# Output products of six batches in seven block products instead of eight, and one order table for the whole program

## The chip, the cores and the metric

One core of a Trainium2 chip runs the kernel. The metric is the device time of one execution in microseconds. Before the change it is 711.71 us, the median of three runs (711.54 to 712.73). All data is float32.

## What is computed

Attention through a few packed tokens (32 per head and batch), and behind it a feed-forward layer of two matrix products with a SiLU between them:

```python
# q, k, v: (8, 8, 576, 64); p: (8, 8, 32, 64): batch, head, token, head dim
def sm_attn(qq, kk, vv):
    s = scale * np.matmul(qq, kk.transpose(0, 1, 3, 2))
    s = s - np.max(s, axis=-1, keepdims=True)
    a = np.exp(s)
    a = a / (np.sum(a, axis=-1, keepdims=True) + 1e-09)
    return np.matmul(a, vv)
p_packed = sm_attn(p, k, v)
x = sm_attn(q, p_packed, p_packed)      # then as (8 * 576, 512)
h = x @ w_in                            # w_in: (512, 2048)
return (h / (1 + np.exp(-h))) @ w_out   # w_out: (2048, 512)
```

## The kernel before, in words

The second attention and the first product are never formed apart: `Packs` multiplies the 32 packed tokens of each head with `w_in` (`pw`, per batch and quarter of the 2048 hidden features), and the shares of the second softmax (`a2`, lines 437 to 447) times `pw` are then the hidden values. `h_products` (L502) does this for one **unit**, a batch and 128 hidden features, over the 576 tokens, in two matmuls of 288 columns (a half batch each) times six.

Six, because every factor is split in two parts, `hi` (rounded to the TensorE's float32r) and `lo` (what is left), and a product is made of three terms, hi·hi, lo·hi and hi·lo. The splitting is work of ScalarE (`hi`) and VectorE (`lo`).

`h_values` (L520 to L522) applies SiLU from PSUM: L520 writes `g`, L521 the same rounded as `g_hi`, L522 the last 32 tokens of each half (the **rest**, `REST`) to the tile `rest`. `h_lower` (L527) makes `g_lo`. `out_products` (L529 to L559) multiplies a unit's 512 main tokens, as four stationary blocks of 128 tokens, with the unit's 128 rows of `w_out`: 4 blocks x 3 terms = 12 matmuls of 512 columns, L534. The sums over a batch's 16 units stand in PSUM (`ps_acc`, two tiles of two banks, one tile for each half batch); `out_rows` copies them out (L580) and stores them. The 64 rest tokens of a batch wait until two batches give 128; four rest units of their own then take 48 matmuls of 512 columns.

The weights arrive as int64 words and are turned into float32 in the first part of the program (`Weights`, L190 to L215, on ScalarE, VectorE and GpSimd).

What sets the order: every engine runs its own list. Up to batch 1 (**the early part**, 32 units) the list is the table `ORDER`; from batch 2 on (**the main loop**, line 690) it is code: `hidden_up_to(u + 2)` makes the hidden values two units ahead of the output products, and `STEPS_AT` puts the steps of the next batch's attention between them. Loads and stores are all issued in order by the queue of SP.

Of the kernel before, what the change touches and what calls it, by code (L numbers as in the profile page):

```python
# [19 lines left out]
P = 128  # L20
# [8 lines left out]
NJ = 4  # L29
JW = DFF // NJ  # L30
# [15 lines left out]
CHUNKS += [(j * FJ + f, 2, inner) for j in range(1, NJ) for inner in (True, False) for f in (0, 2)]  # L46
PLACES = ["new", "last", "new", "last", 8, 10, 12, 14]
# [4 lines left out]
W6 k0 as0.0 wf0 wf1 ws0 W1 as0.1 am0.0 am0.1 v0 ax0.0 ax0.1 wz0 wj0 W7 at0.0 at0.1 ws1 ay0.0 ay0.1 wz1 wj1 wf2 ar0  # L52
W5 aa0 an0 wu1 wl1 W1 ai0 aj0 q0 W1 aS0.0 ws2 pp0 wz2 wj2 wf3 aC0.0 pu0 pl0 W1 aB0.0 aM0.0 ws3 wz3 aS0.1 aC0.1 pp1
wf4 aX0.0 wf5 pu1 wj3 ws5 wf6 W4 aB0.1 aM0.1 ws4 aD0.0 W13 aU0.0 aX0.1 aD0.1 wf7 ws7 wz7 pl1 k1 aH0.0 wu3 aU0.1 ws6
aH0.1 as1.0 ac1.0 wj7 v1 aL0.0 aL0.1 as1.1 ac1.1 wl3 h0.0 wz5 wj5 h0.1 am1 g0.0 g0.1 l0.0 h1.0 h1.1 l0.1 ax1.0 ax1.1
wz4 wj4 q1 at1.0 wu5 wl5 at1.1 g1.0 g1.1 ar1 l1.0 o0.0 wz6 wf8 o0.1 wf9 wf10 pp2 pu2 pl2 ws8 l1.1 o1.0 h2.0 h2.1 wj6
wz8 g2.0 ay1 l2.0 g2.1 pp3 pu3 pl3 wj8 wu7 wl7 ws9 l2.1 o1.1 wz9 wj9 h3.0 h3.1 g3.0 g3.1 l3.0 wf11 o2.0 o2.1 ws10
aa1 wf12 wf13 pp4 pu4 wz10 wj10 l3.1 ws11 wu10 an1 o3.0 o3.1 pl4 ai1 h4 aj1 wz11 wl10 g4 l4 h5 ws12 aS1.0 aT1.0
aM1.0 g5 aX1.0 wj11 o4 l5 aS1.1 aT1.1 aD1.0 h6 g6 k2 l6 wu11 h7 o5 wl11 aH1.0 aL1.0 o6 pp5 aM1.1 g7 aX1.1 pu5 l7
# [701 lines left out]
```

## Time and profile before

| | |
|---|---|
| median of the runs | 711.71 us |
| span of the profiled execution | 713.2 us |
| early part, up to the last output product of batch 1 | some 199 us |
| main loop, batches 2 to 7 | some 510 us |
| PE busy | 98% |
| VectorE and ScalarE busy | 47% each |
| moved by DMA | 65.20 MB |

PE is TensorE's matmul row, PEld its weight load, DVE VectorE, ACT ScalarE, POOL GpSimd, SP the engine that issues the loads. A matmul's duration in the profile contains its way through the array and overlaps the next, so that the distance from one start to the next tells its cost, and a long run of equal matmuls gives that distance as its length over their number. The profiled execution's span is 1.5 us above the median of the runs.

### The profile page before, as it was taken

The numbers are of one execution on the slowest core, as the hardware profiler recorded it, in microseconds if no ns is written. First come the engines' busy times: TensorE is split into PE (matmuls) and PEld (weight loads), VectorE is DVE, ScalarE is ACT, GpSimd is POOL, SyncE is SP. The second block draws the span as 40 slices with busy tenths as digits, with TensorE's granted clock in tenths as the row PEclk, the third lists the DMA queues.
The fourth block names the chain that finished last, engine by engine and source line by source line (L and its number), as shares of the span: only waits on it lengthen the run. The fifth ranks groups of instructions, "written<-read, shape, count | busy, mean of one in ns | idle before, by whom it ended". The sixth has DMA issues, their size and how long they took to land.

```text
span 713.2 us, 12182 instructions
## 1 busy us (share of the span) xinstructions
PE 696.0 (98%) x5094; PEld 571.3 (80%) x5094; DVE 333.6 (47%) x506; ACT 331.7 (47%) x619; POOL 17.0 (2%) x16
## 2 busy tenths in 40 slices
PE   7889999999999999999999999999999999999997
PEld 5667788878868887888878888888878888888886
DVE  4889876677353336332462324523462234622112
ACT  4778776555333516352442524453253532533221
POOL 0102002020000000000000000000000000000000
PEclk9789999999999999999999999999999999999999
DMA  9666452613032130212211122031401210010002
GB/s 360 269 239 248 158 206 84 247 82 119 1 133 82 33 146 1 82 58 91 74 60 38 58 91 74 11 116 35 145 1 59 82 34 2 1 60 0 1 1 74
DMA packets 30869, 65.20 MB, mean 91 GB/s; under 512 B 19296, under 2 KB 19296, under 8 KB 26464
## 3 DMA queue, kind: packets, MB, share of 16 engines
q1 hardware_dynamic: 30720, 64.30, 24.8%
q8 instruction: 40, 0.66, 0.4%
q10 hardware_dynamic: 96, 0.13, 0.1%
q14 instruction: 13, 0.11, 0.0%
HBM read 48.76 MB, written 11.53 MB: 85 GB/s over the span
## 4 chain that ended last, share of the span: by engine, by line
PE 88%; DVE 5%; ACT 2%; DMA 2%; issue 1%; POOL 0%; SPq 0%; ACTq 0%; DVEq 0%
PE ps_acc L534 54%; PE ps_two L502 27%; PE ps_two L222 6%; DMA w_raw<-in_w_out 1%; PE ps_two L320 1%; DMA w_raw<-in_w_in 1%; DVE w_raw L196 1%; DVE w_raw L195 1%; DVE win L202 1%; ACT w_raw L191 0%; DVE win L196 0%; ACT L520 0%; DVE wo_lo L215 0%; DVE g_lo L527 0%; ACT w_raw L190 0%
## 5 line engine op out<-in xcount | busy, mean ns | idle before, releaser
L534 PE MATMUL ps_acc<-wo_hi,g_hi 128*128 128x512 f32 x576 | 229.6, 399 | 0.0
L534 PE MATMUL ps_acc<-wo_lo,g_hi 128*128 128x512 f32 x576 | 225.9, 392 | 0.9 <-DVE wo_lo L215 0.9
L534 PE MATMUL ps_acc<-wo_hi,g_lo 128*128 128x512 f32 x576 | 225.5, 392 | 0.0
L527 DVE TENSOR_TENSOR g_lo<-g,g_hi 128x512 fp32r<-128x512 f32 (+1 forms) x132 | 88.6, 672 | 263.3 <-ACT g_hi L521 263.3
L520 ACT ACTIVATE g<-ps_two 128x512 f32<-128x512 f32 (+1 forms) x132 | 77.4, 587 | 267.0 <-PE ps_two L502 243.2
L502 PE MATMUL ps_two<-a_hi,pw_hi 128*128 128x288 f32 x512 | 153.3, 299 | 0.1
L502 PE MATMUL ps_two<-a_lo,pw_hi 128*128 128x288 f32 x512 | 152.6, 298 | 0.0
L502 PE MATMUL ps_two<-a_hi,pw_lo 128*128 128x288 f32 x512 | 151.7, 296 | 0.0
L534 PEld LDWEIGHTS ps_acc<-wo_hi,g_hi 128*128 128x128 f32 x576 | 108.3, 188 | 40.7 <-issue 21.0
L534 PEld LDWEIGHTS ps_acc<-wo_hi,g_lo 128*128 128x128 f32 x576 | 108.4, 188 | 24.1 <-DVE g_lo L527 0.5
L534 PEld LDWEIGHTS ps_acc<-wo_lo,g_hi 128*128 128x128 f32 x576 | 108.4, 188 | 19.7 <-DVE wo_lo L215 1.2
L502 PEld LDWEIGHTS ps_two<-a_hi,pw_hi 128*128 128x128 f32 x512 | 97.5, 190 | 6.1 <-ACT tm L248 0.9
L502 PEld LDWEIGHTS ps_two<-a_lo,pw_hi 128*128 128x128 f32 x512 | 97.2, 190 | 3.4
L502 PEld LDWEIGHTS ps_two<-a_hi,pw_lo 128*128 128x128 f32 x512 | 97.3, 190 | 0.0
L521 ACT ACTIVATE g_hi<-ps_two 128x512 fp32r<-128x512 f32 (+1 forms) x132 | 76.6, 581 | 9.4 <-PE ps_acc L534 9.4
L474 DVE TENSOR_TENSOR pw_lo<-ps_two,pw_hi 128x1024 fp32r<-128x1024 f32 (+1 forms) x35 | 38.5, 1127 | 14.6 <-ACT pw_hi L471 14.6
L471 ACT CAST pw_hi<-ps_two 128x1024 fp32r<-128x1024 f32 (+1 forms) x35 | 31.9, 943 | 24.2 <-PE ps_two L222 24.2
L222 PE MATMUL ps_two<-win,ppT 64*32 64x512 f32 (+1 forms) x560 | 33.5, 568 | 4.2 <-ACT rest L522 2.4
L522 ACT ACTIVATE rest<-ps_two 128x64 f32<-128x64 f32 (+1 forms) x132 | 30.4, 230 | 0.0
L222 PEld LDWEIGHTS ps_two<-win,ppT 64*32 64x32 f32 x560 | 8.2, 108 | 18.4 <-issue 10.8
L520 ACT ACT_TABLE_LOAD x17 | 21.8, 1283 | 2.0 <-PE ps_two L502 1.8
L190 ACT ACTIVATE w_raw<-w_raw 128x1024 int32<-128x1024 uint32 (+1 forms) x13 | 13.3, 1022 | 8.0 <-DMA w_raw<-in_w_in 5.5
(104 smaller groups left out, 445.9 us busy)
## 6 DMA issues: line engine op xcount, KB each, us to landing
kvq_t<-in_v SPq DMA_DIRECT2D x8, 1280.0 KB, 5.9
kvq_t<-in_pkT SPq DMA_DIRECT2D x7, 1216.0 KB, 7.3
out<-o SPq DMA_DIRECT2D x16, 512.0 KB, 2.8
kvq_t<-in_qT SPq DMA_DIRECT2D x7, 1152.0 KB, 5.0
w_raw<-in_w_in SPq DMA_DIRECT2D x6, 1024.0 KB, 7.0
win<-in_w_out SPq DMA_DIRECT2D x3, 1024.0 KB, 4.6
w_raw<-in_w_out SPq DMA_DIRECT2D x3, 1024.0 KB, 7.4
tm<-tm SPq DMA_DIRECT2D x56, 40.0 KB, 1.9
```

Of the source, the lines that this page charges most:

```text
L190: nc.scalar.activation(low, low.bitcast(U32), AF.Copy, scale=2.0**-29)
L195: nc.vector.tensor_scalar(up.bitcast(F32), up.bitcast(F32), TOP, -TOP, op0=ALU.min, op1=ALU.max)
L196: nc.vector.scalar_tensor_tensor(low, up, -(2**31), low, op0=ALU.bitwise_and, op1=ALU.bitwise_or)
L222: nc.tensor.matmul(bank(par)[NP * i : NP * i + NP], lhs(r, i), rhs(r, i), start=True, stop=True)
L471: nc.scalar.copy(self.hi, self.ps[:, :, : self.nf * P])
L474: nc.vector.tensor_tensor(self.lo, self.ps[:, :, : self.nf * P], self.hi.bitcast(F32), ALU.subtract)
L502: nc.tensor.matmul(bank, p[:, par, cols], a[:, par], start=(n == 0), stop=(n == len(todo) - 1))
L520: nc.scalar.activation(g, ps[..., :MAIN], AF.Silu)
L521: nc.scalar.activation(g_hi, ps[..., :MAIN], AF.Silu)
L522: nc.scalar.activation(to, ps[..., MAIN:HS], AF.Silu)
L527: nc.vector.tensor_tensor(g_lo[:, c], g[:, c], g_hi[:, c].bitcast(F32), ALU.subtract)
L534: nc.tensor.matmul(bank, g[:, rows], w[:, f], start=(first and n == 0), stop=(last and n == 2))
```

## The change

**Seven products.** For batches 2 to 7 a unit is now a half batch (256 main tokens) and a pair of 128 features. Its output product is seen as a 2 x 2 block product: two blocks of tokens by two blocks of features, times two blocks of features by two halves of 256 output columns. `pair_products` makes it with seven block products (Strassen's scheme, in the variant with four sums on each side) where the plain form has eight: 7 x 3 = 21 matmuls of 256 columns in place of 12 of 512. What goes with it:

- On the hidden values: ScalarE writes SiLU once (`pair_values`, 512 wide, and `rest_values`), GpSimd adds four sums of blocks to it (`pair_sums`, three instructions of 128, 256 and 128 columns), and `all_upper` and `all_lower` split seven blocks, 896 columns, in place of four. L521 goes away.
- On the weights: four sums per pair of features are made once in the early part (`pair_of_w`, two VectorE adds of 512 columns; `sums_of_pair`, four GpSimd instructions of 256; `sums_upper` and `sums_lower`, 1024 wide on ScalarE and VectorE), for eight pairs, and are stored to HBM. The first of them goes in the place of a part of `w_out` (`first_in_place`); the other three are read again for every unit (`load_sums`, 786 KB, four buffers, 96 times).
- In PSUM: the seven products are summed over the pairs of a half batch in four banks, `ps_acc0` to `ps_acc3`, of which there is one set. `pair_rows` joins them to the output: one ScalarE copy of 256 columns and five VectorE adds (512, 256, 256, 256 and 512). The rest units use banks 0 and 2, and `rest_rows` joins these.
- `win`, the first weights, no longer stays in SBUF: it is stored once (`w_in32`, 4 x 1 MB), and 22 quarters of 1 MB are fetched again (`Packs.fetch`).

**One table.** `ORDER` now holds the whole program, and the loop over the units is gone. Steps are cut finer (`clip`, `shift`, `scaled2`, ...), with the same instructions. The new table differs from the old from the first steps on; its rows say little to a reader, and two of its lines stand here:

```python
O41 O42 N43 I43 F43 L43 N44 B45 N45 S45 aa3 S46 G45 B46 an3 ai3 aj3 I44 F44 O43 L44 N46 E2.0 S48 G46 I45 F45 L45 B47
O139 F140 L140 E7.1 O140 F141 L141 F142 O141 F143 L142 L143 O142 O143 Y6
```

(O output products, B hidden products, G SiLU, N SiLU of the rest, I sums, F hi, L lo, S load of the weights' sums, E and Y the joining of the banks; the number is the unit's.)

```diff
+    w_in32 = tc.dram_tile((NJ, P, FJ * DM), I32, name="w_in32")
+    sums_of_w = tc.dram_tile((NPAIR, P, 2, 3 * HALF), F32, name="sums_of_w")
+    first_sums = tc.dram_tile((NPAIR, P, 2, HALF), F32, name="first_sums")
...
+    def pair_values(u):
+        g = hidden[u] = gp_main.tile([P, 8 * P], F32, name="g")
+        nc.scalar.activation(g[:, : 4 * P].rearrange("p (e s) -> p e s", e=2), made["h", u, None][..., :MAIN], AF.Silu)
...
+    def pair_sums(u):
+        x = hidden[u].rearrange("p (n x) -> p n x", x=P)
+        one = x[:, 1:2].broadcast_to([P, 2, P])
+        nc.gpsimd.tensor_tensor(x[:, 4], x[:, 0], x[:, 2], ALU.subtract)
+        nc.gpsimd.tensor_tensor(x[:, 5:7], x[:, 0:5:4], one, ALU.subtract)
+        nc.gpsimd.tensor_tensor(x[:, 7], x[:, 3], x[:, 6], ALU.add)
...
+    def all_upper(u):
+        g = all_of(u)
+        both = [gp_main.tile([P, 7 * P], F32R, name=name)[:, : g.shape[1]] for name in ("g_hi", "g_lo")]
+        hidden[u] = g, *both
+        nc.scalar.copy(both[0], g)
+    def all_lower(u):
+        g, g_hi, g_lo = hidden[u]
+        nc.vector.tensor_tensor(g_lo, g, g_hi.bitcast(F32), ALU.subtract)
...
+    def terms(out, g_hi, g_lo, at, w_hi, w_lo, first=False, last=False):
+        rows = slice(at * P, at * P + P)
+        todo = ((g_hi, w_hi), (g_hi, w_lo), (g_lo, w_hi))
+        for n, (g, w) in enumerate(todo):
+            nc.tensor.matmul(
+                out, g[:, rows], w, start=(first and n == 0), stop=(last and n == 2), skip_group_check=True
...
+    def pair_products(u):
+        b, (hf, p) = units[u]
+        g_hi, g_lo = hidden[u][-2:]
+        last = p == NPAIR - 1
+        def term(bank, cols, at, w_hi, w_lo):
+            key = "pair", b, hf, bank
+            begun = opened.get(key)
+            opened[key] = True
+            terms(acc[bank][:, cols], g_hi, g_lo, at, w_hi, w_lo, not begun, last)
+        f1, f2 = 2 * p, 2 * p + 1
+        x = summed_tiles.pop((b, hf, p))
+        t = lambda n: (x[:, 0, n * HALF : n * HALF + HALF], x[:, 1, n * HALF : n * HALF + HALF])
+        w = lambda f, c: (wo_hi[:, f, c], wo_lo[:, f, c])
+        term(1, low, 5, *t(0))
+        term(1, high, 2, *w(f2, low))
+        term(0, low, 0, *w(f1, low))
+        term(0, high, 4, *t(2))
+        term(2, low, 6, *w(f2, high))
+        term(3, low, 1, *t(1))
+        term(3, high, 3, *w(f1, high))
...
+    def load_sums(u):
+        b, (hf, p) = units[u]
+        x = summed_tiles[b, hf, p] = tp.tile([P, 2, 3 * HALF], F32R, name="sums_of_w")
+        nc.sync.dma_start(x.bitcast(F32), sums_of_w[p])
...
+    def sums_of_pair(p):
+        b11, b21, b22, b12 = (made["r", p][:, n * HALF : n * HALF + HALF] for n in range(4))
+        nc.gpsimd.tensor_tensor(b22, b12, b22, ALU.add)
+        nc.gpsimd.tensor_tensor(b12, b12, b11, ALU.subtract)
+        nc.gpsimd.tensor_tensor(b11, b11, b22, ALU.subtract)
+        nc.gpsimd.tensor_tensor(b21, b11, b21, ALU.add)
...
+    def first_in_place(p):
+        for n, t in enumerate((wo_hi, wo_lo)):
+            nc.sync.dma_start(t[:, 2 * p, high].bitcast(F32), first_sums[p, :, n])
+        summed[p] = True
...
+    def rest_rows(b):
+        o = osb.tile([P, 2, DM], F32, name="o")
+        if opened.get(("rest", b, 0)):
+            nc.scalar.copy(o[:, 1], acc[0])
+            nc.vector.tensor_tensor(o[:, 0], acc[2], o[:, 1], ALU.add)
+            nc.vector.tensor_tensor(o[:, 0, high], o[:, 0, high], o[:, 1, low], ALU.add)
...
+    def pair_rows(b, hf):
+        o = osb.tile([P, 2, DM], F32, name="o")
+        o4 = o.rearrange("p k (c x) -> p (k c) x", x=HALF)
+        banks = [x.rearrange("p (c x) -> p c x", x=HALF) for x in acc]
+        twice = lambda n: o4[:, n : n + 1].broadcast_to([P, 2, HALF])
+        add = lambda to, ps, x: nc.vector.tensor_tensor(to, ps, x, ALU.add)
+        nc.scalar.copy(o4[:, 1], banks[0][:, 0])
+        add(o4[:, 0:3:2], banks[1], twice(1))
+        add(o4[:, 1], banks[0][:, 1], o4[:, 0])
+        add(o4[:, 3], banks[3][:, 1], o4[:, 0])
+        add(o4[:, 3], banks[2][:, 0], o4[:, 3])
+        add(o4[:, 0:2], banks[3], twice(1))
+        store(b, hf, o)
```

Three places show how it moves instructions. On PE, at the end of a unit's output products in the main loop, there stood before (a plain form: ahead of the arrow what is written, behind it first the moving and then the stationary factor; `wo` is `w_out`, `pw` the packed tokens times `w_in`):

```order
L534 MATMUL ps_acc<-wo_hi,g_hi 128x512
L534 MATMUL ps_acc<-wo_lo,g_hi 128x512
L534 MATMUL ps_acc<-wo_hi,g_lo 128x512
L502 MATMUL ps_two<-a_hi,pw_hi 128x288
L502 MATMUL ps_two<-a_lo,pw_hi 128x288
L502 MATMUL ps_two<-a_hi,pw_lo 128x288
```

and now, for one unit (`ps_acc_2184` is bank 1, `2183` bank 0, `2185` bank 2; `sums_of_w` are the loaded sums of weights):

```order
L587 MATMUL ps_two<-a_hi,pw_lo 128x288
L643 MATMUL ps_acc_2184<-sums_of_w,g_hi 128x256 x2
L643 MATMUL ps_acc_2184<-sums_of_w,g_lo 128x256
L643 MATMUL ps_acc_2184<-wo_hi,g_hi 128x256
L643 MATMUL ps_acc_2184<-wo_lo,g_hi 128x256
L643 MATMUL ps_acc_2184<-wo_hi,g_lo 128x256
L643 MATMUL ps_acc_2183<-wo_hi,g_hi 128x256
L643 MATMUL ps_acc_2183<-wo_lo,g_hi 128x256
L643 MATMUL ps_acc_2183<-wo_hi,g_lo 128x256
L643 MATMUL ps_acc_2183<-sums_of_w,g_hi 128x256 x2
L643 MATMUL ps_acc_2183<-sums_of_w,g_lo 128x256
L643 MATMUL ps_acc_2185<-wo_hi,g_hi 128x256
```

The matmuls of 512 columns became more matmuls of 256, each with its own stationary block, over four banks that all units of a half batch share.

On VectorE at the end of the program there stood before (`o` is the staged output):

```order
L527 TENSOR_TENSOR g_lo_6452<-rest_93,g_hi_6451 128x512
L580 COPY o_6470<-ps_acc_5986 128x1024
L527 TENSOR_TENSOR g_lo_6474<-rest_93,g_hi_6473 128x512
L527 TENSOR_TENSOR g_lo_6491<-rest_93,g_hi_6490 128x512
L569 COPY o_6530<-ps_acc_6477 128x256
```

and now:

```order
L637 TENSOR_TENSOR g_lo<-rest,g_hi 128x512
L785 TENSOR_TENSOR o<-ps_acc_2184,o 128x2x256
L785 TENSOR_TENSOR o<-ps_acc_2183,o 128x256
L785 TENSOR_TENSOR o<-ps_acc_2186,o 128x256
L785 TENSOR_TENSOR o<-ps_acc_2185,o 128x256
L785 TENSOR_TENSOR o<-ps_acc_2186,o 128x512
L637 TENSOR_TENSOR g_lo<-rest,g_hi 128x512 x3
L770 TENSOR_TENSOR o<-ps_acc_2185,o 128x512
L771 TENSOR_TENSOR o<-o 128x256
```

The joining of a half batch's four banks, five adds, now stands between the first and the second splitting of the last rest tokens, and the last copy of 256 columns became an add of 512 and one of 256.

On the queue of SP, in the loop over the batches, there stood before (`kvq_t` takes the inputs of the next batch's attention, `tm` the turned scores):

```order
L143 DMA kvq_t_4073<-in_pkT 128x2432
L162 DMA kvq_t_4147<-in_v 128x2560
L583 DMA out<-o_4427 128x2x512
L583 DMA out<-o_4430 128x2x512
L156 DMA kvq_t_4488<-in_qT 128x2304
L299 DMA tm_4588<-tm_4585 32x5x64 x2
L299 DMA tm_4588<-tm_4585 32x4x64 x2
```

and now:

```order
L714 DMA sums_of_w_3126<-sums_of_w_104 128x1536
L714 DMA sums_of_w_3183<-sums_of_w_104 128x1536
L714 DMA sums_of_w_3185<-sums_of_w_104 128x1536
L714 DMA sums_of_w_3263<-sums_of_w_104 128x1536
L216 DMA kvq_t_3265<-in_v 128x2560
L532 DMA w_quarter_3273<-w_in32_103 128x2048
L714 DMA sums_of_w_3280<-sums_of_w_104 128x1536
L714 DMA sums_of_w_3319<-sums_of_w_104 128x1536
L764 DMA out<-o_3343 128x2x512
L210 DMA kvq_t_3357<-in_qT 128x2304
L714 DMA sums_of_w_3372<-sums_of_w_104 128x1536
L714 DMA sums_of_w_3444<-sums_of_w_104 128x1536
```

Loads of the weights' sums and of the first weights' quarters stand between the others, so that a load or a store that waits holds up the sums behind it.

## Rows read from the trace of the kernel before

**Rows 1.** The page's first two parts: busy time and share of the span of three engines, and the granted clock of PE in 40 slices (tenths).

```profile
PE 696.0 (98%) x5094; PEld 571.3 (80%) x5094; DVE 333.6 (47%) x506; ACT 331.7 (47%) x619; POOL 17.0 (2%) x16
...
PEclk9789999999999999999999999999999999999999
```

**Rows 2.** The chain that ended last, by engine.

```profile
PE 88%; DVE 5%; ACT 2%; DMA 2%; issue 1%; POOL 0%; SPq 0%; ACTq 0%; DVEq 0%
```

**Rows 3.** Windows by stage: length, busy time of each engine (and its instructions), granted clock, DMA share, GB/s.

```profile
0.00:32.00 32.00, 25.31 (x319) 18.50 (x319) 21.93 (x44) 18.84 (x35) 3.81 (x9) 0.89 0.81 329
32.00:80.00 48.00, 45.24 (x389) 34.72 (x375) 43.23 (x72) 38.11 (x68) 5.20 (x3) 0.89 0.58 217
80.00:199.00 119.00, 117.05 (x805) 97.19 (x812) 77.69 (x101) 70.00 (x116) 7.95 (x4) 1.00 0.35 126
199.00:709.00 510.00, 508.40 (x3605) 420.89 (x3589) 190.32 (x290) 204.34 (x401) 0.00 (x0) 1.00 0.17 57
```

**Rows 4.** Who waited for whom, PE alone: us in total, times, longest; the two longest of ten rows.

```profile
PE ps_two L222 <- ACT rest L522: 3.4, 2, 2.4
PE ps_acc L392 <- DVE tm L425: 1.9, 2, 1.2
```

**Rows 5.** Pieces of the chain in order of time: start, length, what, how many.

```profile
210.63 2.73 PE ps_acc L534 x12
...
226.09 3.19 PE ps_two L502 x24
...
364.68 10.95 PE ps_acc L534 x48
...
689.89 19.09 PE ps_acc L534 x84
```

**Rows 6.** Timeline of PE at 22.6 us: start, length from the first start to the last end, 26 passes of 128 columns, each behind a weight load of its own.

```profile
22.60 3.07 PE L137 MATMUL ps_two<-ident 128*128 128x128 f32 x26
```

**Rows 7.** Windows of the first slice and of that stretch, columns as in Rows 3.

```profile
0.00:17.83 17.83, 13.19 (x199) 9.88 (x199) 8.85 (x21) 8.24 (x16) 1.74 (x7) 1.00 0.91 359
22.60:25.60 3.00, 3.00 (x28) 2.88 (x26) 2.83 (x6) 3.00 (x6) 1.04 (x1) 1.00 1.01 426
```

**Rows 8.** Groups of instructions by line and form: shapes, number, busy us, mean ns of one, idle time before.

```profile
L527 DVE TENSOR_TENSOR g_lo<-g,g_hi 128x512 fp32r<-128x512 f32 x124 | 85.4, 688 | 262.5 <-ACT g_hi L521 262.5
L520 ACT ACTIVATE g<-ps_two 128x512 f32<-128x512 f32 x124 | 74.3, 599 | 262.6 <-PE ps_two L502 241.3 <-DVE g_lo L527 21.1
...
L474 DVE TENSOR_TENSOR pw_lo<-ps_two,pw_hi 128x1024 fp32r<-128x1024 f32 x31 | 36.9, 1219 | 13.2 <-ACT pw_hi L471 13.2
...
L471 ACT CAST pw_hi<-ps_two 128x1024 fp32r<-128x1024 f32 x31 | 30.4, 1016 | 24.0 <-PE ps_two L222 24.0
L522 ACT ACTIVATE rest<-ps_two 128x64 f32<-128x64 f32 x124 | 28.7, 231 | 0.0
L520 ACT ACT_TABLE_LOAD x17 | 21.8, 1283 | 2.0 <-PE ps_two L502 1.8
...
L569 DVE COPY o<-ps_acc 128x256 f32<-128x256 f32 x4 | 1.7, 424 | 11.5 <-ACT o L568 11.5
...
L568 ACT COPY o<-ps_acc 128x256 f32<-128x256 f32 x4 | 1.5, 372 | 12.4 <-PE ps_acc L534 12.4
```

**Rows 9.** Timeline of VectorE and GpSimd in two stretches (a GpSimd add of 1024 columns alone, and one beside VectorE).

```profile
106.88 1.89 POOL L203 TENSOR_TENSOR w_raw<-w_raw 128x1024 int32<-128x1024 int32 x1 [35.54 <-DVE w_raw L202]
...
144.25 0.68 DVE L527 TENSOR_TENSOR g_lo<-g,g_hi 128x512 fp32r<-128x512 f32 x1
...
144.42 2.27 POOL L203 TENSOR_TENSOR w_raw<-w_raw 128x1024 int32<-128x1024 int32 x1 [26.50 <-DVE w_raw L202]
145.21 2.03 DVE L195 TENSOR_SCALAR w_raw<-w_raw 128x1024 f32<-128x1024 f32 x1 [0.28 <-ACT w_raw L191]
```

**Rows 10.** DMA: one queue's packets, MB and share of the 16 engines' span; then issues by line: number, KB each, median us from issue to landing.

```profile
q1 hardware_dynamic: 30720, 64.30, 24.8%
...
out<-o SPq DMA_DIRECT2D x16, 512.0 KB, 2.8
...
w_raw<-in_w_in SPq DMA_DIRECT2D x6, 1024.0 KB, 7.0
...
win<-in_w_in SPq DMA_DIRECT2D x2, 512.0 KB, 13.3
```

**Rows 11.** Timeline of the last 5 us.

```profile
708.58 0.39 PE L534 MATMUL ps_acc<-wo_hi,g_lo 128*128 128x512 f32 x1
709.05 0.37 ACT L568 COPY o<-ps_acc 128x256 f32<-128x256 f32 x1 [7.81 <-PE ps_acc L534]
709.46 0.42 DVE L569 COPY o<-ps_acc 128x256 f32<-128x256 f32 x1 [7.49 <-ACT o L568]
709.91 0.80 SPq L573 DMA_DIRECT2D out<-o  x2
```

More of the change, by code (lines that the diff above doesn't have):

```diff
@@ new lines, in pair_sums, with all_of @@
+    def pair_sums(u):
[4 more added lines that the diff above has]
+        nc.gpsimd.tensor_tensor(x[:, 7], x[:, 3], x[:, 6], ALU.add)
+    def all_of(u):
+        b, f, *more = units[u]
+        if more:
+            return rest[:, f : f + FJ].rearrange("p f e h s -> p (f e h s)")
+        return hidden[u][:, P:]
@@ L529, in products @@
     def products(bank, u, f, at, first, last):
         g_hi, g_lo = hidden[u][-2:]
-        rows = slice(at * P, at * P + P)
-        todo = ((g_hi, wo_hi), (g_hi, wo_lo), (g_lo, wo_hi))
-        for n, (g, w) in enumerate(todo):
-            nc.tensor.matmul(bank, g[:, rows], w[:, f], start=(first and n == 0), stop=(last and n == 2))
+        terms(bank, g_hi, g_lo, at, wo_hi[:, f], wo_lo[:, f], first, last)
     def is_last(u):
-        return u + 1 == len(units) or units[u + 1][0] != units[u][0] or len(units[u + 1]) > len(units[u])
+        if u >= n_early:
+            return units[u][0:1] != units[u + 1][0:1] or len(units[u]) != len(units[u + 1]) if u + 1 < len(units) else True
@@ L539, in first_of @@
+        return units[u + 1][0] != units[u][0]
     def first_of(u):
@@ new lines, in packed_attention_ffn, with rest_products @@
+    low, high = slice(0, HALF), slice(HALF, DM)
+    def rest_products(u):
+        b, f, _ = units[u]
+        first, last = f == 0, f + FJ == NF
+        for n in range(FJ):
+            bank = 0 if n % 2 == 0 and (f + n) // 2 in summed else 2
+            begun = opened.get(("rest", b, bank))
+            opened["rest", b, bank] = True
+            products(acc[bank], u, f + n, n, not begun, last and n >= FJ - 2)
+    opened = {}
+    def pair_products(u):
[18 more added lines that the diff above has]
+        term(3, high, 3, *w(f1, high))
@@ L561, in out_rows @@
     def out_rows(u, h):
         b, f, *more = units[u]
-        sums = acc[first_of(u), h]
-        if more:
-            o = osb.tile([P, 2, DM], F32, name="o")
-            half = DM // 2
-            nc.scalar.copy(o[:, 0, :half], sums[:, 0, :half])
-            nc.vector.tensor_copy(o[:, 0, half:], sums[:, 0, half:])
-            for n, (e, h) in enumerate((e, h) for e in range(2) for h in range(2)):
-                at = (b + e) * S + h * HS + MAIN
-                rows = slice((2 * e + h) * REST, (2 * e + h) * REST + REST)
-                (nc.scalar if n % 2 and b == B - 2 else nc.sync).dma_start(out[at : at + REST], o[rows, 0])
-            return
+        banks = sums[first_of(u), h]
@@ L632, in packed_attention_ffn @@
-    gp_b = ent(tc.tile_pool(name="gp_b", bufs=1))
-    done = n_early
-    def hidden_up_to(u):
-        nonlocal done
-        while done < min(u, len(units) - 1):
-            done += 1
-            if len(units[done]) == 2:
-                h_products(done)
-            h_values(done)
-            h_lower(done)
-    def packs_in(b, *quarters):
-        both = [Packs(b, FJ * j, FJ) for j in quarters]
-        for part in both:
-            part.products()
-        for part in both:
-            part.upper()
-            part.lower()
@@ L720, in _laid_out @@
+    for step in ORDER.split():
+        which = step.rstrip("0123456789.") if step[0] != "Z" else step
+        steps[which](*map(int, filter(None, step[len(which) :].split("."))))
 def _laid_out(q, k, v, p, moe_w_in, moe_w_out):
```

391 lines of the change are left out of this document (224 added, 167 removed).

## The prediction, made before the changed kernel ran

> **What bounds the kernel now.** I read the page's busy times first, then the chain, then windows by stage. PE is busy 98% of the span, VectorE and ScalarE 47% each [rows 1], and 88% of the chain that ended last is PE [rows 2]. A busy PE row proves little, since matmuls overlap; so I look at who PE waited for. Its longest wait in total is 3.4 us, and the next 1.9 us [rows 4], all in the first part of the program. From 80 us on the granted clock is 1.00, the higher of the two levels (2.4 GHz), and in the main loop (199 to 709 us) PE is busy 508.4 of 510 us while VectorE works 190.3, ScalarE 204.3 and GpSimd nothing [rows 3]. The main loop is bound by PE alone: it gets shorter only if matmuls take less time, and work on the other engines is free as long as it stays ahead of PE. The first 80 us are different: there VectorE works 43.2 of 48 us and the clock is 0.89 [rows 3].
>
> **What a matmul costs.** A long run of 512 columns takes 10.95 us for 48, one unit's output products 2.73 us for 12, so 0.228 us each; 24 matmuls of 288 columns take 3.19 us, 0.133 us each [rows 5]. The difference of 0.095 us for 224 columns is 0.00042 us a column, and 288 columns at that price leave 0.011 to 0.013 us that each matmul pays whatever its width. A matmul of 256 columns is not in the trace of before. By this line it takes 0.133 - 32 x 0.00042 = 0.1194 us. From above, it can't take longer than one of 288 columns, 0.133 us, unless width is not what counts. Between these lies the weight load: each of the 26 passes of 128 columns at 22.6 us has its own load, and they come every (3.07 - 0.3) / 25 = 0.111 us at a clock of 1.00 [rows 6, 7]. By the line, 128 columns would take only 0.066 us, so there something else sets the pace, which may be the load. If a load of 0.111 us and the fixed 0.013 us were added, a matmul of 256 columns would take 0.124 us. I take 0.1194, since two rows of the same kind of matmul lie on either side of a line that has no bend between them, and keep 0.124 and 0.133 for the range.
>
> The Trainium skill ("TensorE: Matmul & The Clock Gate", Back-to-back issue gap) gives N / 2.4 + 2.5 ns for the gap, 109 ns at 256 and 216 ns at 512 columns; by that the change would save 96 x (12 x 0.2157 - 21 x 0.1092) = 28 us. The trace's 0.228 us at 512 columns speaks against it. The same page (LDWEIGHTS) puts a load of 128 columns at 128 / 1.2 = 107 ns, which is as long as 256 columns at full clock, and so speaks against narrow matmuls here; the 0.111 us between the passes agree with it.
>
> **The change, part by part.**
>
> 1. *Output products of batches 2 to 7.* For each pair of features and half batch, 96 units: before 12 x 0.2275 = 2.73 us, now 21 x 0.1194 = 2.51 us. That is 0.223 us a unit and **-21.4 us** in all, on PE, where it counts. At 0.124 it is 96 x (2.73 - 2.604) = -12.1 us, at 0.133 it is +6 us; the break-even lies at 0.130 us. One block product in eight is saved, 12.5%, but the fixed 0.013 us now falls due 21 times instead of 12, which takes 0.12 us back. Hidden products, rest units, packs and attention keep their matmuls.
>
> 2. *The other engines in the main loop.* A unit used to need 599 + 593 (L521, like L520) + 231 ns of ScalarE and 688 ns of VectorE [rows 8]. Now ScalarE does 599 + 231 ns and a split of 896 columns, about 0.91 us from the 1016 ns for 1024; VectorE splits 896, about 1.09 us from 688 and 1219 for 512 and 1024 [rows 8]. GpSimd adds 512 columns in three steps, 1.0 us and some tenths from its 1.89 us for 1024 [rows 9], if float adds cost what those of integers do. A unit with its hidden products (12 x 0.133 = 1.6 us) lasts 4.1 us on PE. Loads of about 1.7, 1.1 and 1.2 us fit with ease; with attention the sums are some 47 us of ScalarE and 46 us of VectorE in a batch of 82 us. So nothing becomes the bound by its sum. What can bite is the order: `g_hi` and `g_lo` have two buffers, so `all_upper` of unit u + 2 can't start before the output products of u are done; then 0.91 + 1.09 us and the signals have to fit under those of u + 1 (2.51 us) and often a hidden product (1.6 us). Without the latter, 2.3 to 2.4 us stand against 2.51: just enough. An exponential with its two table loads (2 x 1.28 us [rows 8]) between two such steps is late by some tenths. Eight more table loads, 34 to 42 by the program, are 10 us of ScalarE in this shadow. I set **+3 us** (bounds 0 and 96 x 0.5 = 48).
>
> 3. *GpSimd beside VectorE.* A GpSimd add of 1024 took 1.89 us alone and 2.27 us when L527, whose two inputs both lie in SBUF, overlapped its start; L527 itself took its usual 0.68 us; L195, which came behind, took 2.03 us [rows 9]. So a GpSimd step may be longer by 0.4 us next to a split. The chain SiLU, sums, hi, lo is some 3.8 us, and two units ahead PE has 6.6 us of other work. I add nothing.
>
> The Trainium skill ("GPSIMD Engine Reference", its first table) says that GpSimd shares its SBUF interfaces with VectorE, with contention for instructions with two SBUF inputs. Here it was GpSimd that paid, not L527.
>
> 4. *The ends of the 12 half batches.* There is now one set of four banks. After the last output product of a half, a copy of 0.37 us and an add of 512 columns (0.69 us) free bank 1, which the next half writes first; the rest follows at 0.42 us a step, faster than the next products reach the banks (0.72 us each). In the table a hidden product of 1.6 us stands between for 11 of the 12, so they cost nothing. Without such a cover each costs 1.2 us. The last one has none, and the rest units begin with bank 0, which is free after 0.37 + 0.69 + 0.42 us and signals: **+1.8 us**.
>
> 5. *The end.* The last copies, 0.37 and 0.42 us [rows 11], become a copy of 512, an add of 512 and one of 256: 0.6 us (between 372 and 1016 ns for 256 and 1024) + 0.69 + 0.42 us, **+0.9 us**.
>
> 6. *Loads.* Sums of 786 KB for each of 96 units, 75.5 MB, and 22 quarters, 23 MB. In a batch 12.6 + 4.2 MB come to the 5.5 MB of inputs, scores and output: 22.3 MB in 82 us, 272 GB/s. Queue 1 moved 64.30 MB in 24.8% of the span, which makes 363 GB/s for a fully busy set of engines, and in the first 17.8 us it ran at 359 GB/s at a share of 0.91 [rows 7, 10]. So the engines are busy three quarters of the time, with four buffers, three units or 12 us ahead. A load of 512 KB took 2.8 us when the queue was short, one of 1 MB 7.0 us, and 13.3 us at the start with everything queued [rows 10]. The order of SP holds sums behind waiting stores and fetches, but mostly with spare tiles already there. I set 0, and keep the other end as a rival. What I looked for and didn't find is PE slowed by DMA: at a share of 1.01 the passes in rows 6 came at full pace [rows 7].
>
> 7. *The early part.* Eight pairs of weight sums add 8 x (2 x 0.69 + 1.22) = 20.8 us of VectorE, 8 us of ScalarE, 16 us of GpSimd. From 80 to 199 us VectorE has 119 - 77.7 = 41 us free [rows 3], so this fits, closer than before. The other order may win or lose in the first 80 us: PE stood idle 2.8 of the 48 us after 32 us, and 11% of clock is missing there [rows 3], 8 us in all. The first attention has the same VectorE steps ahead of it. I set **+2 us** (bounds -8 and +20.8).
>
> Sum against the profiled execution: 713.2 - 21.4 + 3 + 1.8 + 0.9 + 2 = 699.5 us of span. The median of the runs lies 1.5 us under that execution's span, so **698.0 us**.
>
> **Rivals.**
>
> *The weight load sets the pace* (0.124 us a matmul). For it speaks the 0.111 us in rows 6; against it that the two widths in rows 5 share one line. Item 1 becomes -12.1 us: 713.2 - 12.1 + 7.7 - 1.5 = 707 us. The LDWEIGHTS section of the Trainium skill's page named above stands for this rival.
>
> *The chain behind each unit eats the gain.* If the splits come 0.23 us late on average, item 1 is gone. For it speaks the 2.4 against 2.51 us of item 2; against it the many hidden products in between. 712 to 722 us, in the middle 717.
>
> *The sums come late, and the kernel is slower.* If sums and fetches don't get 272 GB/s, DMA sets the pace from batch 2 on. For it speaks that landings took up to 13.3 us when much was queued [rows 10]; against it that 217 GB/s needed only a share of 0.58 [rows 3], 374 at a full one. At 250 GB/s a batch takes 89 us in place of 82, six times, some 42 us: 740 us. It decides from a landing of 12 us, three units.
>
> *The table also repairs the early part.* If the 8 us of item 7 come back and the splits are never late: about 688 us.
>
> *The change does not do what it says* can be left aside: the program has 2016 matmuls of 256 columns in place of 1152 of 512.
>
> **How the numbers follow.** The forecast has a chance of 0.62 (692 to 703 us, other terms of item 2 and 7); the weight load 0.12 (703 to 709); the late splits 0.10; late sums 0.06; the repaired early part 0.10 (686 to 692). The range of 690 to 712 us leaves out late sums, half of the late splits and a part of the last. A measurement of this kernel can tell 0.2%, 1.4 us, from no change. Slower than 713.1 us: late sums and 0.06 of the late splits, 0.12. Within: the other 0.04 of these. Faster than 710.3: 0.84.
>
> **What would show it.** The starts of matmuls of 256 columns 0.119 us apart show item 1 right, 0.124 or more the weight load. A main loop with PE waiting for `g_hi` or `g_lo` at L643 in total over 5 us shows item 2 wrong; waits for `sums_of_w`, item 6. One wait of near 2 us for bank 0 before the last rest units, and 5.2 us from the last matmul to the end, are items 4 and 5. The early part should still end at about 200 us. I am wrong if the narrow matmuls don't follow the line, or if PE waits often and shortly, which no sum of busy times shows.

## The result and the profile after

The changed kernel takes 695.88 us, the median of four runs (694.97 to 696.58), beside 712.21 us for the kernel before on the same chip (711.54 to 712.73): a ratio of 0.977, with a 95% interval of 0.9756 to 0.9784. The prediction was 698.0 us, in a range of 690 to 712.

The page's busy times, its main DMA queue and the chain by engine, which answer to [rows 1, 2, 10], then the groups of GpSimd's sums (number, busy us, mean ns, idle before) and the loads of the weights' sums (number, KB each, median us to landing):

```profile
PE 674.6 (97%) x5958; PEld 593.1 (85%) x5958; DVE 425.9 (61%) x588; ACT 386.5 (56%) x641; POOL 232.4 (33%) x336
...
q1 hardware_dynamic: 54944, 177.56, 69.0%
...
PE 77%; DVE 10%; ACT 4%; DMA 4%; SPq 2%; issue 2%; POOL 1%; ACTq 0%; DVEq 0%
...
L619 POOL TENSOR_TENSOR g<-g 128x128 f32<-128x128 f32 x96 | 56.4, 587 | 290.7 <-ACT g L609 290.6
...
L620 POOL TENSOR_TENSOR g<-g 128x256 f32<-128x256 f32 x96 | 75.0, 783 | 6.6
...
L621 POOL TENSOR_TENSOR g<-g 128x128 f32<-128x128 f32 x96 | 52.3, 546 | 6.6
...
sums_of_w<-sums_of_w SPq DMA_DIRECT2D x96, 768.0 KB, 6.3
```

PE is still the bound, but its share of the chain fell from 88 to 77%, although its busy share hardly changed. VectorE, ScalarE and DMA now stand in the chain in many pieces, most of them short: PE has no long wait, but much has to come just in time.

Windows by stage (length, busy time of each engine and its instructions, granted clock, DMA share, GB/s), beside [rows 3]:

```profile
32.00:80.00 48.00, 46.59 (x408) 36.24 (x408) 43.86 (x73) 38.41 (x70) 5.21 (x3) 0.98 0.63 222
80.00:200.00 120.00, 117.77 (x804) 95.04 (x810) 98.83 (x118) 72.77 (x118) 40.95 (x36) 1.00 0.67 241
200.00:690.00 490.00, 487.05 (x4469) 446.09 (x4453) 259.35 (x351) 254.74 (x419) 182.02 (x288) 1.00 0.70 260
```

The early part ends where it did, now with VectorE busy 98.83 of 120 us. The main loop is some 20 us shorter with PE still full. DMA moves 260 GB/s at a share of 0.70, close to what item 6 worked out (272 and three quarters). From 32 to 80 us the granted clock is 0.98 in place of 0.89.

Who PE waited for (us in total, times, longest; the longest row and two of the output products), and below it a row of PE's weight loads (PEld):

```profile
PE ps_acc L456 <- DVE tm L506: 3.4, 2, 2.7
...
PE ps_acc L643 <- DVE g_lo L605: 2.0, 3, 1.3
...
PE ps_acc L643 <- DVE o L785: 0.8, 1, 0.8
```

```profile
PEld ps_acc L643 <- DVE g_lo L637: 0.3, 1, 0.3
```

L605 is the split of the early part. For L637, the split of the seven blocks, PE has no row of waiting at all and its weight loads have one wait of 0.3 us; for the joining of the banks (`o` of L785) PE has a single one.

Pieces of the chain in the main loop (start, length, what), which answer to [rows 5]:

```profile
221.50 4.97 PE ps_acc L643 x42
...
231.80 3.20 PE ps_two L587 x24
```

Two units' products, 42 matmuls of 256 columns, take 4.97 us, 0.1183 us each. The hidden products beside them cost what they did, 0.133 us.

The last half batch's end and the end of the program, in the timeline:

```profile
677.34 0.37 ACT L786 COPY o<-ps_acc 128x256 f32<-128x256 f32 x1 [0.92 <-PE ps_acc L643]
...
677.75 2.60 DVE L785 TENSOR_TENSOR o<-ps_acc,o 128x512 f32<-128x512 f32 x5 [0.60 <-ACT o L786]
...
678.09 0.28 PE L643 MATMUL ps_acc<-wo_hi,g_lo 128*128 128x256 f32 x1
...
679.09 0.19 PEld L643 LDWEIGHTS ps_acc<-wo_hi,g_hi 128*128 128x128 f32 x1 [0.92 <-ACT g_hi L633]
679.12 0.47 PE L643 MATMUL ps_acc<-wo_hi,g_hi 128*128 128x512 f32 x1 [0.75 <-DVE o L785]
...
689.66 0.59 ACT L769 COPY o<-ps_acc 128x512 f32<-128x512 f32 x1 [4.36 <-PE ps_acc L643]
...
689.91 0.39 PE L643 MATMUL ps_acc<-wo_hi,g_lo 128*128 128x512 f32 x1
...
690.40 0.69 DVE L770 TENSOR_TENSOR o<-ps_acc,o 128x512 f32<-128x512 f32 x1 [4.38 <-PE ps_acc L643]
691.12 0.42 DVE L771 TENSOR_TENSOR o<-o 128x256 f32<-128x256 f32 x1
```

Both joinings begin before PE's last matmul: bank 0 is complete while PE still fills banks 2 and 3 (at the very end bank 2), so its copy (677.34, 689.66) is hidden.

### The profile page after: what moved, and what is told of

Read it like the earlier page. It is cut to its first block, busy times and chain, and to the rows that moved or that the text cites. A ratio compares the mean times of both kernels' runs of the same rounds, so it can differ in the third digit from the quotient of the medians.

```text
span 694.8 us, 14721 instructions
## 1 busy us (share of the span) xinstructions
PE 674.6 (97%) x5958; PEld 593.1 (85%) x5958; DVE 425.9 (61%) x588; ACT 386.5 (56%) x641; POOL 232.4 (33%) x336
## 4 chain that ended last, share of the span: by engine, by line
PE 77%; DVE 10%; ACT 4%; DMA 4%; SPq 2%; issue 2%; POOL 1%; ACTq 0%; DVEq 0%
PE ps_acc L643 46%; PE ps_two L587 24%; PE ps_two L284 5%; DMA win<-in_w_out 2%; PE ps_two L384 2%; DMA sums_of_w<-sums_of_w 2%; SPq L363 2%; DVE tm L420 1%; DVE g_lo L605 1%; DVE w_raw L249 1%; DVE w_raw L253 1%; DVE g_lo L637 1%; DVE wo_lo L277 1%; DVE o L785 1%; DVE win L261 0%
## 5 line engine op out<-in xcount | busy, mean ns | idle before, releaser
L637 DVE TENSOR_TENSOR g_lo<-g,g_hi 128x896 fp32r<-128x896 f32 x96 | 106.4, 1116 | 131.2 <-ACT g_hi L633 128.4
L643 PE MATMUL ps_acc<-wo_hi,g_hi 128*128 128x256 f32 (+1 forms) x576 | 185.1, 321 | 0.8 <-DVE o L785 0.8
L643 PE MATMUL ps_acc<-wo_hi,g_lo 128*128 128x256 f32 (+1 forms) x576 | 183.9, 319 | 2.0 <-DVE g_lo L605 2.0
L643 PE MATMUL ps_acc<-wo_lo,g_hi 128*128 128x256 f32 (+1 forms) x576 | 183.6, 319 | 0.0
L619 POOL TENSOR_TENSOR g<-g 128x128 f32<-128x128 f32 x96 | 56.4, 587 | 290.7 <-ACT g L609 290.6
L633 ACT CAST g_hi<-g 128x896 fp32r<-128x896 f32 x96 | 89.8, 940 | 76.7 <-POOL g L621 45.0
L643 PEld LDWEIGHTS ps_acc<-wo_hi,g_hi 128*128 128x128 f32 x576 | 108.4, 188 | 16.3 <-issue 5.6
L643 PE MATMUL ps_acc<-sums_of_w,g_hi 128*128 128x256 f32 x576 | 116.7, 284 | 0.3 <-DMA sums_of_w<-sums_of_w 0.3
L643 PEld LDWEIGHTS ps_acc<-sums_of_w,g_hi 128*128 128x128 f32 x576 | 89.1, 189 | 9.3 <-issue 7.8
L643 PE MATMUL ps_acc<-sums_of_w,g_lo 128*128 128x256 f32 x288 | 81.2, 282 | 0.0
L620 POOL TENSOR_TENSOR g<-g 128x256 f32<-128x256 f32 x96 | 75.0, 783 | 6.6
L621 POOL TENSOR_TENSOR g<-g 128x128 f32<-128x128 f32 x96 | 52.3, 546 | 6.6
```

What stands on the lines that cost most here:

```text
L619: nc.gpsimd.tensor_tensor(x[:, 4], x[:, 0], x[:, 2], ALU.subtract)
L620: nc.gpsimd.tensor_tensor(x[:, 5:7], x[:, 0:5:4], one, ALU.subtract)
L621: nc.gpsimd.tensor_tensor(x[:, 7], x[:, 3], x[:, 6], ALU.add)
L633: nc.scalar.copy(both[0], g)
L637: nc.vector.tensor_tensor(g_lo, g, g_hi.bitcast(F32), ALU.subtract)
L643: nc.tensor.matmul(out, g[:, rows], w, start=(first and n == 0), stop=(last and n == 2), skip_group_check=True)
```

## The experiments

Each kernel is the changed one with the edit shown. The time before it is compared with is that of the same chip (712 to 713 us). Theory: the narrow matmuls bring the gain, and the rest of the work has room beside PE. Rivals: the weight load sets the pace, or the work around the products is the price.

**e1. Plain products, all the other work kept.** The sums, the splits of seven blocks and the loads stay; only T, which puts the first sums in place of weights, is left out, so that the plain products have the plain weights. They don't read the sums. They use two banks, which two copies empty in place of the copy and five adds (not in the cut shown).

```diff
-        term(1, low, 5, *t(0))
...
-        term(3, high, 3, *w(f1, high))
+        for k in range(2):
+            for e, f in enumerate((f1, f2)):
...
+                terms(acc[2 * k], g_hi, g_lo, 2 * e + k, wo_hi[:, f], wo_lo[:, f], not begun, last and e == 1)
```

> The changed kernel with the plain block products back: 12 matmuls of 512 columns for each pair of features and half batch in place of 21 of 256, in two of the four banks, which two copies empty. All other work of the change is kept (sums of hidden values on GpSimd, splits of 896 columns, weight sums made, stored and loaded for every unit), though the products don't use the sums; only the putting of the first sum in the place of w_out is left out. Theory (PE alone bounds the main loop, the gain is in the matmuls): 96 x (12 x 0.2275 - 21 x 0.1196) = 21 us more than the changed kernel's 695.9, so 717 us (714 to 720). Rival (the new table brings the gain): 696 us, as with the change.

Measured: 719.18 us (718.98 to 719.84), 1.010 of before (1.0078 to 1.0122). That is 23.3 us over the changed kernel. **The matmuls bring the whole gain, and more.**

**e2. Plain products alone**, in the same table, without the sums of values and of weights and their loads, and with splits of four blocks.

```diff
+        if step.rstrip("0123456789.") in ('T', 'S', 'r', 'R', 'ru', 'rl', 'rk', 'I'):
+            continue
```

> The changed kernel's table with the plain products and none of the extra work: no sums on GpSimd, splits of 512 columns, no weight sums made or loaded. What is left of the change is the table, the cut in half batches and pairs, and the fetching of the first weights. Theory (the extra work lies beside PE and costs nothing): as with the plain products and all extra work, 717 us, within 3 us, so 714 to 717. Rival (the extra work or the loads cost time in the main loop or in the early part, which the matmuls then repay more than they show): clearly less, 705 us or under. Against the kernel before it tells what the table alone does: the theory has it within 5 us of 711.7, the rival that the table brings the gain has 696.

Measured: 716.16 us (715.97 to 716.55), 1.0055 (1.004 to 1.0071). So all the extra work costs 3.0 us where PE has its old matmuls beside it, and the table without the seven products is slower than the old program. Windows of the main loop of e1 and then e2, columns as above:

```profile
200.00:712.00 512.00, 509.21 (x3578) 419.67 (x3571) 235.80 (x299) 256.78 (x418) 182.59 (x288) 1.00 0.65 246
```

```profile
200.00:712.00 512.00, 507.62 (x3565) 418.30 (x3563) 190.41 (x298) 224.44 (x416) 0.00 (x0) 1.00 0.27 97
```

In the timelines I read where the last output product of batch 1 starts (the early part), the last output product of all (the main loop), and the span's end. The lines of the early part, for before, e2, e1 and after, and of the main loop, for e2 and e1 (before and after: [rows 11] and 689.91 above):

```profile
198.40 0.39 PE L534 MATMUL ps_acc<-wo_hi,g_lo 128*128 128x512 f32 x1
```

```profile
195.65 0.39 PE L643 MATMUL ps_acc<-wo_hi,g_lo 128*128 128x512 f32 x1
...
709.81 0.39 PE L643 MATMUL ps_acc<-wo_hi,g_lo 128*128 128x512 f32 x1
```

```profile
198.08 0.39 PE L643 MATMUL ps_acc<-wo_hi,g_lo 128*128 128x512 f32 x1
...
712.66 0.39 PE L643 MATMUL ps_acc<-wo_hi,g_lo 128*128 128x512 f32 x1
```

```profile
199.14 0.39 PE L643 MATMUL ps_acc<-wo_hi,g_lo 128*128 128x512 f32 x1
```

| kernel | early part, us | main loop, us | behind it, us | span, us |
|---|---|---|---|---|
| before | 198.4 | 510.2 | 4.7 | 713.2 |
| e2, table, plain products | 195.7 | 514.2 | 4.5 | 714.3 |
| e1, and all other work | 198.1 | 514.6 | 4.5 | 717.2 |
| after | 199.1 | 490.8 | 4.9 | 694.8 |

From row to row: the table's own main loop +4.0 us (with the half batches and the fetches of the first weights, which e2 keeps), the extra work in the main loop +0.4, the seven products -23.8. The early part can't be read row by row, since each row is a single execution. In all listed runs the time lies 1.7 to 1.9 us above the span, so the profiled execution of before took some 715.0 us, 2.8 above the median, and its granted clock was 0.987, where most runs of that kernel show 0.990 to 0.998. By the medians e2 is 3.9 us longer than before, which its main loop alone explains; e1 is 6.9 longer, 4.4 of them in the main loop. So the order of the table neither won nor lost in the early part, as far as this tells, and the weights' sums took some 2.7 us there. The kernels with these sums, after and all the experiments but e2, end the early part between 198.0 and 199.5 us.

**e3. The 256 columns in two matmuls of 128.**

```diff
+            parts = [slice(0, wide)] if wide > HALF else [slice(0, P), slice(P, HALF)]
+            for m, c in enumerate(parts):
...
+                    out[:, c], g[:, rows], w[:, c], start=(first and n == 0 and m == 0), stop=(last and n == 2),
```

> The changed kernel with each matmul of 256 columns cut in two of 128: 42 in place of 21 for a unit, each with its own weight load, the same columns in all. Theory (a matmul costs its columns and 0.013 us): 42 x 0.0664 = 2.79 us a unit in place of 2.51, 27 us in all, 723 us (717 to 730). Rival (the weight load of 0.111 us sets the pace below some width): 42 x 0.111 = 4.66 us a unit, 2.15 more, 206 us in all, 902 us (880 to 920).

Measured: 905.29 us (904.7 to 905.88), 1.271 (1.2687 to 1.2733). The rival holds at 128 columns. A piece of its chain:

```profile
351.47 9.33 PE ps_acc L646 x84
```

9.33 / 84 = 0.111 us, the price of the passes of [rows 6], where the line through 512 and 288 columns gives 0.066. The line ends between 128 and 256 columns; at 256 it still holds, 0.007 us above that floor. Each matmul here has a weight load of its own; whether that load sets the floor or another cost of a matmul, e3 does not separate.

**e4, e8, e9. VectorE's split done twice, wholly or in part**: 896, 448 and 128 columns more per unit (the edit of e8; in e4 the whole line stands in a loop of two). The rest units have the same line and so the same added work.

```diff
+        nc.vector.tensor_tensor(g_lo[:, :448], g[:, :448], g_hi[:, :448].bitcast(F32), ALU.subtract)
         nc.vector.tensor_tensor(g_lo, g, g_hi.bitcast(F32), ALU.subtract)
```

> The changed kernel with the splitting of the seven blocks' lower part on VectorE done twice (same result), 1.1 us more VectorE for each of the 96 units, on the way from the hidden values to the output products, and twice for the rest units too. Theory (the chain behind a unit has slack: a hidden product stands between two output products in most places, and VectorE has a third of its time free): PE waits only where none stands between, about ten places, 0.9 us each, and where attention's steps pile up: 700 to 712 us. Rival (the chain is just late already): 1.1 x 96 = 107 us, 800 us.

> VectorE splits the first 448 columns of each unit a second time, some 0.62 us more per unit (688 ns for 512 columns), 60 us over 96 units. The whole split done twice cost 43.6 us for some 107. Theory: each unit has a slack of some tenths of a us and only what lies beyond it counts, so that half the delay costs far less than half: 697 to 708 us. Rival: there is no slack, and about 40% of any delay reaches PE: 696 + 24 = 720 us (715 to 725).

> VectorE splits the first 128 columns of each unit a second time, some 0.28 us more per unit (from 424 ns for 256 columns and 688 for 512), 27 us over 96 units. Theory of the slack: 695 to 699 us. Rival, 40% of any delay reaches PE: 696 + 11 = 707 us (704 to 710).

Measured: e4 739.53 us (738.08 to 740.9), 1.0382 (1.036 to 1.0405). e8 715.68 (714.83 to 716.65), 1.0033 (1.0021 to 1.0045). e9 703.78 (703.71 to 704.43), 0.9869 (0.9844 to 0.9894). By these ratios against 0.977, times 712 us, the three cost 44, 19 and 7 us. Groups of e9, e8 and e4 (number, busy us, mean ns), the added split, of e4 both in one:

```profile
L637 DVE TENSOR_TENSOR g_lo<-g,g_hi 128x128 fp32r<-128x128 f32 x96 | 31.2, 325 | 110.8 <-ACT g_hi L633 107.8 <-PE ps_two L587 2.7
```

```profile
L637 DVE TENSOR_TENSOR g_lo<-g,g_hi 128x448 fp32r<-128x448 f32 x96 | 63.7, 664 | 95.8 <-ACT g_hi L633 90.2 <-PE ps_acc L644 3.2 <-PE ps_two L587 2.1
```

```profile
L638 DVE TENSOR_TENSOR g_lo<-g,g_hi 128x896 fp32r<-128x896 f32 x192 | 221.3, 1158 | 86.7 <-ACT g_hi L633 80.0 <-PE ps_acc L644 2.8
```

With the gap of 0.1 us the smallest delay is 0.43 us a unit, 41 us in all, of which 7 reached the end; of 0.77 us (73) it was 19, of 1.16 us (111) it was 44: 17, 25 and 39%. e4 fell between theory and rival, e8 at the lower edge of its rival's range, e9 just under its rival's. There is no slack that all units share, as the theory wanted, nor does a fixed 40% count. Some units have no room for 0.43 us, and with each further step more of them run out. The weight loads' waits for the split in e9, e8 and e4 show it:

```profile
PEld ps_acc L644 <- DVE g_lo L638: 3.3, 10, 0.8
```

```profile
PEld ps_acc L644 <- DVE g_lo L638: 9.0, 15, 1.3
```

```profile
PEld ps_acc L644 <- DVE g_lo L638: 19.8, 26, 1.8
```

One place in the changed kernel became 10, 15 and 26, and their sums are nearly half of the time lost. The rest has no single row: PE also waits longer for ScalarE's SiLU and for the splits of the packs, which the added work holds up in turn.

**e5. Every load of sums followed by a copy of the same 786 KB inside HBM**, 75 MB more on the same queue.

```diff
         nc.sync.dma_start(x.bitcast(F32), sums_of_w[p])
+        nc.sync.dma_start(again[p], sums_of_w[p])
```

> The changed kernel with the 786 KB of weight sums of each unit copied a second time, from HBM to HBM, to a place that nobody reads: 75 MB more for the DMA engines. They were busy 69% of the span with 177.6 MB, 370 MB in a millisecond at a full share. Theory (loads are hidden as long as the engines have time left): 253 MB take 684 us of all engines, just the length of the kernel, so that waits for the sums begin: 696 to 740 us. Rival (loads are a bound already): in step with the bytes, over 800 us.

Measured: 770.76 us (767.45 to 774.08), 1.0814 (1.0776 to 1.0852), between the two. Its queue, the longest waits of PE, and the window of its main loop:

```profile
q1 hardware_dynamic: 58016, 253.06, 83.6%
```

```profile
PE ps_acc L644 <- DMA sums_of_w<-sums_of_w: 25.0, 15, 3.6
PE ps_two L285 <- DMA w_quarter<-w_in: 14.5, 5, 6.6
```

```profile
200.00:768.00 568.00, 513.62 (x4469) 465.36 (x4453) 260.36 (x352) 255.47 (x419) 178.99 (x288) 0.95 0.90 357
```

The waits are not the whole price. The granted clock of the main loop is 0.95, where the changed kernel has 1.00: about a tenth of these 568 us ran at the lower level (1.2 GHz). PE is busy 513.6 us with the same matmuls that took 487.1; by estimate, up to these 26 of the 75 us are the slower clock's.

**e6. Three buffers for the loaded sums in place of four.**

```diff
-TP_BUFS = 4
+TP_BUFS = 3
```

> The changed kernel with three buffers for the weight sums in place of four: a load can start two units, some 8 to 9 us, ahead of its use and not 12 to 13. The loads took 6.3 us from issue to landing in the median. Theory (four buffers have spare lead): within 3 us of 695.9, with single waits where inputs of the attention are loaded at the same time. Rival (the lead is used up): a wait of 1 to 3 us for most units, 720 us or more.

Measured: 710.71 us (708.21 to 714.55), 0.9972 (0.9952 to 0.9992): most of the gain is gone. Again between the two, nearer to the rival. PE's two longest waits:

```profile
PE ps_two L284 <- DMA w_quarter<-w_in: 4.7, 2, 2.4
PE ps_acc L643 <- DMA sums_of_w<-sums_of_w: 4.5, 3, 2.8
```

By the ratios that is 14 us more than the changed kernel, and the granted clock of the main loop fell a little here too, to 0.99. A buffer less delays not only the sums but, on the one queue of SP, also the quarters behind them. A fifth buffer wasn't tried.

**e7. No hidden product between two half batches**: at 11 places of the table it moves behind the first output products of the next half. One of them, the rest of the table left out:

```diff
-B54 S55 G54 L53 G56 I54 O52
+S55 L53 G56 O52 B54 G54 I54
```

> The changed kernel's table with the hidden products that stand between the last output product of a half batch and the first of the next moved behind that first one, at 11 places; nothing stands between them then at five or six, packs or attention at the others. Theory (the joining of the single set of banks is hidden by these hidden products): PE waits for VectorE's adds out of the banks, 0.5 to 1.2 us at each bare place, and the moved hidden products are later, so the splits behind them may be too: 699 to 708 us. Rival (the four banks are free in time anyway): 696 us, no waits for the adds.

Measured: 720.59 us (718.77 to 722.09), 1.0109 (1.0084 to 1.0134): twice what the theory allowed. Waits of PE (`g_lo` of L574 is the split, `o` of L722 the joining of the banks):

```profile
PE ps_acc L580 <- DVE g_lo L574: 5.5, 3, 2.3
...
PE ps_acc L580 <- DVE o L722: 2.2, 5, 0.8
```

PE's own waits for the bare joining are 2.2 us in five places, at most 0.8 each, less than the 1.2 of item 4. A part of the rest is another thing that the edit did: the hidden product that was moved starts its own chain of SiLU, sums and splits 2.5 us later, and that one was late. A further part is the clock, which fell to the lower level in three stretches of the main loop, 17 us together; one of them, and the stretch ahead of it, in which PE was busy 8.4 of 10.2 us:

```profile
417.60:427.80 10.20, 8.39 (x105) 7.71 (x100) 3.37 (x8) 2.02 (x4) 3.14 (x6) 1.00 0.66 268
427.80:434.60 6.80, 6.06 (x27) 6.07 (x28) 0.68 (x1) 0.00 (x0) 0.00 (x0) 0.50 0.89 300
```

Here 27 matmuls fill 6.06 us, 0.22 each. Half of the 17 us, some 8 of the 25 that e7 lost, is the estimate for it.

## Why the prediction was right, and where by luck

**Item 1, the matmuls: right, a little small.** Forecast -21.4 us by 0.1194 us each; the main loop lost 23.8 us against the same program with plain products, and undisturbed the matmuls came every 0.1183 us. The difference of 0.0011 us times 2016 is 2.2 us. The rival of the weight load was wrong, as the starts at 256 columns show, but the width was near the place where it would have been right: e3 shows a floor of 0.111 us. The Trainium skill ("TensorE: Matmul & The Clock Gate", LDWEIGHTS) gives P / 1.2 ns for a load of P columns, by estimate 107 ns for 128, and e3's 111 ns is close to it; the gap that the same page states for isolated matmuls (Back-to-back issue gap), by estimate 109 ns for 256 columns, is not reached, the trace has 118.

**Items 2 and 3, the other engines: right in sum, wrong in the reason.** I set +3 us for late splits and their neighbours. The extra work cost 0.4 us in the main loop (e2 to e1), and PE's matmuls waited for no split there. The loads of a batch, put at 47 us of ScalarE and 46 of VectorE, were 42.5 and 43.2 (a sixth of the main loop's busy times). But the argument that the loads "fit with ease" and that only sometimes a few tenths are missing did not describe the kernel: e9 shows that 0.43 us more a unit already cost 7 us. The split is not late because the order leaves it just enough in a number of places, not because it has room. The sums on GpSimd, which I put at 1.2 us a unit, take 587 + 783 + 546 ns, 1.92 us, and this too fitted.

**A term that I did not have:** the main loop of the table without the products and the extra work is 4.0 us longer than the old one (e2). Summed from start to start of PE's matmuls in both traces, 1.9 us of it lie behind matmuls of the packs and scores, 1.4 behind those of hidden products and 0.7 behind those of output products. Two rows of e2's waits are part of it, which the old kernel does not have: hidden products that follow a pack wait for VectorE's turning of the scores (L420, five of the six in the main loop), and an output product waits once for the copy out of a bank (L780):

```profile
PE ps_two L587 <- DVE tm L420: 1.5, 6, 0.2
...
PE ps_acc L643 <- DVE o L780: 0.9, 1, 0.9
```

In the old loop no hidden product stood behind packs; in the table ten do. What is left, some 1.9 us, is spread over short gaps, and its cause stays open. It was item 2's +3 us, set for something else, that made up for much of this term.

**Item 4, the half batches' ends: right, the last one too dear.** I counted copy and adds from the unit's last matmul, 1.8 us. The copy began before it, and between the last two matmuls, 678.09 and 679.12, lie 1.03 us where 0.12 would do: 0.9 us. Nor is it the joining's alone: the weight load ahead of that matmul waited until 679.09 for ScalarE's `g_hi` of the rest, so that without the joining it would hardly have been shorter. Without cover PE waits up to 0.8 us for a half's joining (e7), not 1.2.

**Item 5, the end: +0.2 us, not +0.9,** for the same reason: the copy of bank 0 hid under the last matmuls of the other bank.

**Item 6, loads: right at 0, again with less room than I said.** PE waited 0.3 us for sums. The lead was put at three units or 12 us, yet one buffer less cost 14 us (e6). The median landing of 6.3 us was the wrong thing to look at; the least, the median and the longest landing of the 96 loads:

```profile
DMA to landing us min/median/max: 4.0/6.3/12.4
```

The longest is as long as the whole lead, and 12 us was the landing at which I had the rival decide. The loads are issued in order, with fetches of 1 MB and inputs of over 1 MB between the sums, and the lead is there for the worst moments. (The 2.8 us that item 6 gives for a load of 512 KB are those of a store, `out<-o` in [rows 10].)

**Item 7, the early part: right.** I set +2 us. The two traces have +0.7, but that of before is of a long execution. By the medians the change is -16.3 us; -19.4 of them are the main loop and +0.2 the end, which leaves some +2.9 for the early part. That is the price of the weights' sums (some 2.7 by e1); a better order is not shown.

**The sum.** I forecast a change of -13.7 us; it was -16.3. The terms were off by -2.4 (item 1), -2.6 (items 2 and 3), -1.8 (item 4, whose cost stands inside the 23.8), -0.7 (item 5), +0.9 (item 7) and +4.0 for the table, together -2.6. The mechanism that carries the gain is shown, by e1; that a missing term of 4 us changed the sum so little is luck.

**The rivals.** The chain behind each unit ate nothing, the sums came in time, and no repair of the early part is to be seen in the medians, though the two traces differ in the clock from 32 to 80 us. But the experiments tell how near the first two were: with 0.77 us more a unit (e8) or one buffer less (e6) the change would have brought nothing or 0.3%.

## What to carry to other kernels

Fewer products in smaller blocks pay as long as a matmul's width still sets its price: draw the line through two widths of the trace, look for the floor under it (here 0.111 us), and stop above it. A wait that is absent from a trace says nothing of its margin; when a change fills engines that were idle, lengthen one step or take one buffer away, and see from which tenth on the time answers. And when an order is changed together with the work, run the new order with the old work: here it was a loss of 4 us that nothing in the sum of the parts had.

## What the hardware showed

GpSimd's adds and VectorE's splits depend on each other. In the timeline of the changed kernel:

```profile
227.01 0.46 POOL L619 TENSOR_TENSOR g<-g 128x128 f32<-128x128 f32 x1 [4.39 <-ACT g L609]
...
227.55 0.74 POOL L620 TENSOR_TENSOR g<-g 128x256 f32<-128x256 f32 x1
...
227.79 1.44 DVE L637 TENSOR_TENSOR g_lo<-g,g_hi 128x896 fp32r<-128x896 f32 x1 [4.21 <-ACT g_hi L633]
...
228.37 1.19 POOL L621 TENSOR_TENSOR g<-g 128x128 f32<-128x128 f32 x1
...
331.81 1.09 DVE L637 TENSOR_TENSOR g_lo<-g,g_hi 128x896 fp32r<-128x896 f32 x1
```

An add of 128 columns takes 0.46 us alone, and 1.19 us here, where it starts under VectorE's split. The split takes 1.09 us where no add runs when it starts, and 1.44 us here, where it starts under an add. The Trainium skill ("GPSIMD Engine Reference", its first table) says that the two share their SBUF interfaces; here both pay, each where it comes second, and GpSimd by more than the 0.4 us that I had allowed. That only GpSimd pays, as it seemed before [rows 9], does not hold: of the trace's 96 splits of 896 columns, 79 start under no add and take 1.03 to 1.09 us, and of the other 17 most take longer, up to 1.63.
